# Half steps of 128 columns with both signs in one PSUM bank, and block sums on GpSimd, in a fused FFT and cosine-gated feed-forward kernel

## The chip, the cores and the metric

The kernel runs on one core of one Trainium2 chip. A core has TensorE (PE in the profile, with its weight loads listed apart as PEld), VectorE (DVE), ScalarE (ACT), GpSimd (POOL) and SyncE (SP, which issues transfers). Each engine works through its own instructions in the order in which they were written; engines wait for one another through semaphores. Matmuls write to PSUM, which has eight banks of 128 partitions by 512 fp32 values; VectorE and ScalarE read and write PSUM too, GpSimd and transfers only SBUF. The metric is the device time of one execution in microseconds (us), lower is better.

## The reference

```python
def _attn_ref(x) -> np.ndarray:            # x: (8, 3008, 256)
    X = np.fft.fft(x, axis=1)
    X = np.fft.fft(X, axis=2)
    return X.real.astype(np.float32)

def _moe_ref(x, w_in, w_out) -> np.ndarray:  # (24064, 256), (256, 2048), (2048, 256)
    h = x @ w_in
    g = h * np.cos(h)
    return (g @ w_out).astype(np.float32)
```

The result of the first function, as 24064 rows of 256 values, is the input of the second. All is fp32, and the matmuls run in fp32, which the trace records as two passes for each.

## The kernel before

**Transform.** A batch is 3008 rows (47 by 64) of 256 columns. `transform(b)` lays out the work of the Fourier transform of batch `b` over the 48 steps of the batch before it, as a table from step to calls: `load_x` (four pieces), `fold` (sums and differences of column pairs, on GpSimd for all batches but the first, two per chunk of 512 columns), `first_half` (matmuls of a chunk into a bank `pz`, the even part into partitions 0 to 63, the odd part into 64 to 127, and then a few single columns once more with another weight), `store_z` and `load_z` (through DRAM, to turn the data), and `second_half` (four matmuls of 128 columns into a bank `pb`, copied by ScalarE to `pq`; its first row is spread over all partitions as `nb` by two transfers). `pz` of later batches and `pb` use one PSUM bank of their own, tag "fft".

**What a step is.** The output of a batch is made in 6 groups of T = 225 (the first) or 256 positions, and each group in 8 steps of 256 columns of `w_in`, so there are 8 x 6 x 8 = 384 steps. The column transform is folded into the weights `WC` and `WS` (cosine and sine parts). A position and its mirror share the cosine part `e` and differ in the sign of the sine part: one matmul with WC and one with WS give both values of `h`.

A step `s` does, for its two blocks `u` of 128 columns:
- `seed` (ScalarE): starts the bank H with 0.25 plus a weight times `nb`.
- `mm1(s, 0)` (TensorE, WC) adds the even part; `act_e` (ScalarE) saves twice that as `ew`.
- `mm1(s, 1)` (TensorE, WS) adds the odd part: H holds the one sign; `dve_h` (VectorE) makes the other sign, `ew - H`, with positions reversed, in the SBUF tile `h`.
- For each sign: `act_round` (ScalarE, adds a large constant, which rounds), `dve_frac` (VectorE, the fraction), then one `act_sin` (ScalarE) over both signs, and `dve_g` (VectorE) multiplies by `h`.
- `dve_s` (VectorE, three parts) makes four sums and differences of the four blocks (two signs by two `u`) in the tile `S`.
- `mm2` (TensorE): seven matmuls of the blocks and sums with combinations of `w_out` add up in four PSUM banks M over the 8 steps of a group.

At the end of a group `take_m` (ScalarE) copies the M banks to `mr`, `combine_m` (GpSimd, seven products into the four outputs, six instructions and two memsets for T = 225) makes `cb`, and `store_out` transposes 32 by 32 on VectorE and sends the rows out.

**Order.** Nothing is scheduled by a planner: the loop at line 740 writes the instructions of step `t` (`cur`), of `t - 1` (`prev`), `t - 2` (`old`) and `t - LAG`, LAG = 3 (`done`), in the order in which every engine is to take them. On TensorE a step is `mm1(cur, 0)`, four matmuls of `mm2(done)`, `mm1(cur, 1)`, three of `mm2(done)`. On ScalarE it is `act_e`, two seeds for the next step, `act_sin`, and two `act_round`. On VectorE it is two `dve_g`, two `dve_frac` with the first of `dve_s` between them, the second of `dve_s`, `dve_h` and the third of `dve_s`. The table of `transform` and that of the opening come at the end of each step.

**Buffers.** PSUM: one bank "fft", four M, three H. A new tile waits until the last reader of the bank that it takes is done.

Of the kernel before, what the change touches and what calls it, by code (L numbers as in the profile page):

```python
# [107 lines left out]
def kernel(  # L108
# [90 lines left out]
    bank = {"fft": 1, "M": 4, "H": 3}  # L199

    def psum(name, tag="fft"):
        return ppool.tile([128, 512], FP, tag=tag, bufs=bank[tag], name=name)
# [3 lines left out]
    xf0 = [spool.tile([128, 2 * IP * 128], FP, tag="S", bufs=2, name="xf") for _ in range(2)]  # L206
# [3 lines left out]
    def fold(b, c, e):  # L210
        lo = IP * (c % 2)
        xv = xs[b, c // 2].rearrange("r (i d) -> r i d", d=ND)[0 : 2 * N2, lo : lo + IP]
        if b == 0:
            xfs[b, c] = xf0[c % 2]
        elif e == 0:
            xfs[b, c] = spool.tile([128, 2 * IP * 128], FP, tag="xf", bufs=1, name="xf")
# [14 lines left out]
    def first_half(b, c):  # L231

        rows = 2 * N2 if b else 128
        fv = xfs.pop((b, c)).rearrange("r (e c) -> r e c", e=2)[0:rows]
        LE, LO, LE0, LO0 = (L[0:rows, 64 * q : 64 * q + 64] for q in range(4))
        pz = psum("pz", "fft" if b else "M")
        a = 128 if c == 0 else 0
        for e, (w, w0) in enumerate(((LE, LE0), (LO, LO0))):
            rows = slice(64 * e, 64 * e + 64)
            if a:  # L240
                nc.tensor.matmul(
                    pz[rows, 0:128], lhsT=w0, rhs=fv[:, e, 0:128], start=True, stop=True
                )
            nc.tensor.matmul(  # L244
                pz[rows, a:512], lhsT=w, rhs=fv[:, e, a:512], start=True, stop=True
            )
        if a:
            nc.tensor.matmul(
                pz[64:128, 0:1], lhsT=LE0, rhs=fv[:, 1, 0:1], start=True, stop=True
            )  # L250
        nc.tensor.matmul(  # L251
            pz[64:128, a:512:128],
            lhsT=LE,
            rhs=fv[:, 1, a:512:128],
            start=True,
            stop=True,
        )
        tag, n = ("zs", 4) if b or c < 4 else ("pq", 8)
        zs = spool.tile([128, 512], FP, tag=tag, bufs=n, name="zs")
        nc.scalar.copy(out=zs, in_=pz)  # L260
        zss[b, c] = zs
# [28 lines left out]
    def second_half(b, g):  # L290
# [4 lines left out]
        for q in range(4):  # L295
# [5 lines left out]
                start=True,  # L301
                stop=True,
            )
# [26 lines left out]
    def transform(b):  # L330
# [5 lines left out]
        for p in range(4):  # L336
            at(8 * p + (0 if p else 3), load_x, b, p)
            for c, o, f in ((2 * p, 6, 8), (2 * p + 1, 9, 13)):
                at(8 * p + o, fold, b, c, 0)
                at(8 * p + o, fold, b, c, 1)  # L340
                at(8 * p + f, first_half, b, c)
                at(8 * p + f + 1, store_z, b, c)
# [80 lines left out]
    def seed(s):  # L423
        T = s.T
        s.pq, s.nb = ready[s.b, s.grp]
        s.H = psum("H", "H")
        for u in range(2):
            f = 2 * s.fp + u
            nc.scalar.activation(  # L429
                out=s.H[:, u * T : u * T + T],  # L430
                in_=s.nb[:, 0:T],
                func=AF.Copy,
                bias=0.25,
                scale=wn[:, f : f + 1],
            )

    def seed_first(s):
        for u in range(2):
            nc.tensor.matmul(
                s.H[:, u * s.T : u * s.T + s.T],  # L440
                lhsT=wrow[:, 128 * u : 128 * u + 128],
                rhs=s.pq[0:1, s.T : 2 * s.T],
                start=False,
                stop=True,
                skip_group_check=True,
            )

    def mm1(s, e):
        T = s.T
        W = WS if e else WC  # L450
        for u in range(2):
            f = 2 * s.fp + u
            nc.tensor.matmul(  # L453
                s.H[:, u * T : u * T + T],
                lhsT=W[:, 128 * f : 128 * f + 128],
                rhs=s.pq[:, e * T : e * T + T],
                start=False,
                stop=True,
                skip_group_check=True,
            )  # L460

    def act_e(s):
        s.ew = spool.tile([128, 512], FP, tag="ew", bufs=2, name="ew")
        nc.scalar.mul(out=s.ew[:, 0 : 2 * s.T], in_=s.H[:, 0 : 2 * s.T], mul=2.0)  # L464

    def dve_h(s):
        T = s.T
        s.h = spool.tile([128, 512], FP, tag="h", bufs=3, name="h")
        nc.vector.tensor_tensor(  # L469
            out=s.h[:, 0 : 2 * T].rearrange("p (u t) -> p u t", u=2)[:, :, ::-1],  # L470
            in0=s.ew[:, 0 : 2 * T].rearrange("p (u t) -> p u t", u=2),
            in1=s.H[:, 0 : 2 * T].rearrange("p (u t) -> p u t", u=2),
            op=ALU.subtract,
        )

    def side(s, sg):
        T = s.T
        return s.r[:, 2 * T * sg : 2 * T * sg + 2 * T], (s.h if sg else s.H)[:, 0 : 2 * T]

    def act_round(s, sg):  # L480
        if sg == 0:
            s.r = spool.tile([128, 1024], FP, tag="r", bufs=4, name="r")
        r, h = side(s, sg)
        nc.scalar.activation(out=r, in_=h, func=AF.Copy, bias=BIG, scale=1.0)  # L484

    def dve_frac(s, sg):
        r, h = side(s, sg)
        nc.vector.scalar_tensor_tensor(  # L488
            out=r, in0=r, scalar=-BIG, in1=h, op0=ALU.add, op1=ALU.subtract
        )  # L490

    def act_sin(s):
        r = s.r[:, 0 : 4 * s.T]
        nc.scalar.activation(out=r, in_=r, func=AF.Sin, bias=0.0, scale=SIN_SCALE)  # L494

    def dve_g(s, sg):
        r, h = side(s, sg)
        nc.vector.scalar_tensor_tensor(  # L498
            out=r, in0=h, scalar=-0.25, in1=r, op0=ALU.add, op1=ALU.mult
        )  # L500

    def dve_s(s, k):
        T = s.T
        gv = s.r[:, 0 : 4 * T].rearrange("p (q t) -> p q t", q=4)
        if k == 0:
            s.S = spool.tile([128, 1024], FP, tag="S", bufs=2, name="S")
        sv = s.S[:, 0 : 4 * T].rearrange("p (q t) -> p q t", q=4)
        if k == 0:
            nc.vector.tensor_tensor(  # L509
                out=sv[:, 0:2],  # L510
                in0=gv[:, 2:3].to_broadcast([128, 2, T]),
                in1=gv[:, 0:4:3],
                op=ALU.subtract,
            )
        elif k == 1:
            nc.vector.tensor_tensor(out=sv[:, 2], in0=sv[:, 1], in1=gv[:, 0], op=ALU.subtract)  # L516
        else:
            nc.vector.tensor_tensor(out=sv[:, 3], in0=gv[:, 1], in1=sv[:, 2], op=ALU.add)  # L518
# [4 lines left out]
    def mm2(s, part):  # L523
        T = s.T
        key = (s.b, s.grp)
        if s.fp == 0 and part == 0:
            acc[key] = []
            started[key] = set()
        gv = s.r[:, 0 : 4 * T].rearrange("p (q t) -> p q t", q=4)
        sv = s.S[:, 0 : 4 * T].rearrange("p (q t) -> p q t", q=4)  # L530
        todo = (
            (0, wv[:, 0, 0, s.fp], gv[:, 0]),
            (1, wv[:, 1, 0, s.fp], gv[:, 1]),
            (2, vx[:, 3, s.fp], gv[:, 3]),
# [5 lines left out]
        for m, w, a in todo[4:] if part else todo[:4]:  # L540
# [17 lines left out]
    def take_m(s, part):  # L558
        T = s.T
        key = (s.b, s.grp)  # L560
        if part == 0:
            mrs[key] = spool.tile([128, 7 * 256], FP, tag="mr", bufs=1, name="mr")
        mv = mrs[key].rearrange("p (m t) -> p m t", m=7)[:, :, 0:T]
        for k in (2, 3) if part else (0, 1):
            n = 1 if k == 3 else 2
            nc.scalar.mul(
                out=mv[:, 2 * k : 2 * k + n],
                in_=acc[key][k].rearrange("p (m t) -> p m t", m=2)[:, 0:n, 0:T],
                mul=TWO_PI,
            )  # L570

    def combine_m(s):
        T = s.T
        key = (s.b, s.grp)
        acc.pop(key)
        mv = mrs.pop(key).rearrange("p (m t) -> p m t", m=7)[:, :, 0:T]
        cb = spool.tile([128, 7 * 256], FP, tag="cb", bufs=1, name="cb")
        cf = cb.rearrange("p (m t) -> p m t", m=7)
        cv = [cf[:, m, 256 - T : 256] if m in (2, 3) else cf[:, m, 0:T] for m in range(7)]
        if T < 256:  # L580
            nc.gpsimd.memset(cf[:, 0:2, T:256], 0.0)
            nc.gpsimd.memset(cf[:, 2:4, 0 : 256 - T], 0.0)
        tt = nc.gpsimd.tensor_tensor
        tt(out=cv[0], in0=mv[:, 0], in1=mv[:, 1], op=ALU.add)
        tt(out=cv[4], in0=mv[:, 0], in1=mv[:, 5], op=ALU.subtract)
        tt(
            out=cf[:, 5:7, 0:T],
            in0=cf[:, 4:5, 0:T].to_broadcast([128, 2, T]),
            in1=mv[:, 3:5],
            op=ALU.add,  # L590
        )
        tt(out=cv[1], in0=cv[6], in1=mv[:, 6], op=ALU.add)
        tt(out=cv[2], in0=cv[5], in1=mv[:, 2], op=ALU.add)
        tt(out=cv[3], in0=cv[5], in1=mv[:, 4], op=ALU.add)
        outs[key] = cb
# [138 lines left out]
    first = steps[0]  # L734
    first.H = psum("H", "H")
    nc.vector.memset(first.H[:, 0 : 2 * first.T], 0.25)
    second_half(0, 0)
    keep_busy(2, "M", 256)
    first.pq, first.nb = ready[0, 0]
    for t in range(n + LAG + 1):  # L740
        cur, prev, old, done = step(t), step(t - 1), step(t - 2), step(t - LAG)
        if cur:
            if t % per == 0:
# [80 lines left out]
```

## Time and profile before

| | |
|---|---|
| median of 3 runs | 1974.51 us (1973.8 to 1974.56) |
| profiled execution, first to last instruction | 1973.1 us |
| mean granted TensorE clock | 0.999 of full |
| 128x1024 sine on ScalarE (L494) | 320 of 1.055 us |
| seed on ScalarE (L429), 128x256 | 640 of 0.478 us |
| `act_e` on ScalarE (L464), 128x512 | 320 of 0.596 us |
| `dve_g` on VectorE (L498), 128x512, from H in PSUM / from `h` in SBUF | 0.672 / 0.729 us |
| first sum of `dve_s` on VectorE (L509), 128x512 | 0.764 us |
| transfers (all queues) | 88.63 MB, 45 GB/s |

The page lists for each engine its busy time and the share of the span. A row of a group reads: line, engine, operation, tiles as out<-in, shape, how many, then busy time in us and the mean of one in ns, then the idle time before them and who ended it. A timeline row reads: start in us, length, engine, line, operation, tiles and shape, count, and in brackets an idle time and who ended it. The recorded end of a matmul includes its way through the array, so matmuls that follow each other without a gap overlap in the record; the distance between starts tells the rate. The same holds for VectorE and ScalarE, where an instruction starts before the one ahead of it has ended in the record.

### The profile page before, as it was taken

The page shows a single profiled execution, that of the slowest core. Times are in us where ns is not written, and L with a number is a line of the kernel's source. Part 1 is how long each engine was busy: PE and PEld are TensorE (multiplying, and loading weights), DVE is VectorE, ACT ScalarE, POOL GpSimd, SP SyncE. Part 2 cuts the span into 40 slices and gives each one's busy share as a digit, 9 for nine tenths or more (in the row PEclk, how much of TensorE's full clock was granted, in tenths as well). Part 3 has the DMA queues.
Part 4 walks back from the last instruction along what each step waited for, and adds up shares of the span by engine and source line. Part 5 has one row for each costly group of instructions (what it writes and reads, how often), then busy time and mean ns, then how long its engine had stood idle before and what let it go on. Part 6 is the DMA issues. An engine that isn't in the chain of part 4 may idle for free.

```text
span 1973.1 us, 28657 instructions
## 1 busy us (share of the span) xinstructions
PE 1948.9 (99%) x9360; PEld 1702.4 (86%) x9360; DVE 1854.4 (94%) x3209; ACT 1482.7 (75%) x2687; POOL 465.1 (24%) x428
## 2 busy tenths in 40 slices
PE   8999999999999999999999999999999999999998
PEld 4888899888988889888898888988889888898887
DVE  2999989999899998999989999999999999899998
ACT  3777777777777777777877777777777777778775
POOL 1123113221133212223222322123311233112111
PEclk9999999999999999999999999999999999999999
DMA  8413221131212212122122301223022220200000
GB/s 194 100 41 62 41 43 31 40 59 35 43 33 46 51 36 43 38 59 38 34 41 51 63 20 37 45 53 55 19 42 53 43 51 21 47 21 10 19 15 22
DMA packets 176682, 88.63 MB, mean 45 GB/s; under 512 B 103303, under 2 KB 173622, under 8 KB 174902
## 3 DMA queue, kind: packets, MB, share of 16 engines
q1 hardware_dynamic: 176374, 86.68, 21.4%
q8 instruction: 75, 1.23, 0.3%
q14 instruction: 73, 0.60, 0.1%
q10 hardware_dynamic: 160, 0.13, 0.0%
HBM read 49.50 MB, written 37.27 MB: 44 GB/s over the span
## 4 chain that ended last, share of the span: by engine, by line
PE 91%; DVE 5%; DMA 2%; ACT 1%; issue 1%; SPq 0%; DVEq 0%; POOL 0%; ACTq 0%; POOLq 0%
PE M L545 53%; PE H L453 31%; PE pz L244 3%; PE pb L297 2%; DVE r L498 1%; DMA xp<-in_x_dram 1%; DVE S L516 1%; DVE S L509 1%; DVE S L518 1%; DVE h L469 1%; DVE r L488 1%; ACT r L484 0%; PE pw L355 0%; DMA out_dram<-ob 0%; SPq L647 0%
## 5 line engine op out<-in xcount | busy, mean ns | idle before, releaser
L494 ACT ACTIVATE r<-r 128x1024 f32<-128x1024 f32 (+1 forms) x384 | 398.5, 1038 | 303.6 <-DVE r L488 302.7
L545 PE MATMUL M<-S,VX 128*128 128x256 f32 (+1 forms) x2304 | 612.3, 375 | 0.0
L545 PEld LDWEIGHTS M<-S,VX 128*128 128x128 f32 x2304 | 437.8, 190 | 49.9
L453 PE MATMUL H<-pq,WS 128*128 128x256 f32 (+1 forms) x1536 | 390.2, 376 | 11.5 <-ACT ew L464 11.2
L453 PE MATMUL H<-pq,WC 128*128 128x256 f32 (+1 forms) x1536 | 393.9, 379 | 0.5 <-ACT H L429 0.5
L545 PE MATMUL M<-r,w 128*128 128x256 f32 (+1 forms) x1536 | 387.7, 375 | 0.0
L429 ACT ACTIVATE H<-nb,wn 128x256 f32<-128x256 f32 (+1 forms) x766 | 362.9, 474 | 18.0 <-DVE r L498 5.6
L469 DVE TENSOR_TENSOR h<-ew,H 128x512 f32<-128x512 f32 (+1 forms) x384 | 256.8, 669 | 92.5 <-PE H L453 86.5
L453 PEld LDWEIGHTS H<-pq,WS 128*128 128x128 f32 x1536 | 289.3, 190 | 53.9 <-ACT ew L464 20.0
L545 PEld LDWEIGHTS M<-r,w 128*128 128x128 f32 x1536 | 300.7, 197 | 27.0
L488 DVE SCALAR_TENSOR_TENSOR r<-r,h 128x512 f32<-128x512 f32 (+1 forms) x384 | 309.5, 806 | 0.0
L453 PEld LDWEIGHTS H<-pq,WC 128*128 128x128 f32 x1536 | 283.2, 190 | 28.9 <-ACT H L429 0.8
L218 POOL TENSOR_TENSOR xf<-xp 94x508 f32<-94x508 f32 x112 | 165.4, 1497 | 566.0 <-PE pz L251 547.9
L509 DVE TENSOR_TENSOR S<-r 128x512 f32<-128x512 f32 (+1 forms) x384 | 290.2, 756 | 0.1
L498 DVE SCALAR_TENSOR_TENSOR r<-h,r 128x512 f32<-128x512 f32 (+1 forms) x384 | 272.6, 710 | 0.0
L484 ACT ACTIVATE r<-H 128x512 f32<-128x512 f32 (+1 forms) x384 | 222.9, 580 | 55.7 <-DVE h L469 52.7
L464 ACT ACTIVATE ew<-H 128x512 f32<-128x512 f32 (+1 forms) x384 | 225.4, 587 | 50.3 <-PE H L453 43.8
L488 DVE SCALAR_TENSOR_TENSOR r<-r,H 128x512 f32<-128x512 f32 (+1 forms) x384 | 255.1, 664 | 0.0
L498 DVE SCALAR_TENSOR_TENSOR r<-H,r 128x512 f32<-128x512 f32 (+1 forms) x384 | 254.0, 661 | 0.3 <-ACT r L494 0.3
L484 ACT ACTIVATE r<-h 128x512 f32<-128x512 f32 (+1 forms) x384 | 236.2, 615 | 0.0
L545 PE MATMUL M<-S,w 128*128 128x256 f32 (+1 forms) x768 | 225.2, 375 | 0.0
L545 PE MATMUL M<-r,VX 128*128 128x256 f32 (+1 forms) x768 | 225.1, 375 | 0.0
(72 smaller groups left out, 1498.4 us busy)
## 6 DMA issues: line engine op xcount, KB each, us to landing
out_dram<-ob SPq DMA_DIRECT2D x728, 32.0 KB
xp<-in_x_dram SPq DMA_DIRECT2D x56, 256.0 KB
zd<-zs SPq DMA_DIRECT2D x112, 96.0 KB
z<-zd SPq DMA_DIRECT2D x28, 384.0 KB
xp<-in_x_dram SPq DMA_DIRECT2D x56, 120.0 KB
nb<-nd SPq DMA_DIRECT2D x40, 128.0 KB
wr<-in_moe_w_in_dram SPq DMA_DIRECT2D x8, 256.0 KB
w<-in_moe_w_out_dram SPq DMA_DIRECT2D x4, 512.0 KB
```

The lines of the kernel that those rows point to most:

```text
L218: (nc.gpsimd if b else nc.vector).tensor_tensor(out=fv[:, e, :, 1:128], in0=xv[:, :, 1:128], in1=xv[:, :, 255:128:-1], op=ALU.subtract if ...
L244: nc.tensor.matmul(pz[rows, a:512], lhsT=w, rhs=fv[:, e, a:512], start=True, stop=True)
L429: nc.scalar.activation(out=s.H[:, u * T : u * T + T], in_=s.nb[:, 0:T], func=AF.Copy, bias=0.25, scale=wn[:, f : f + 1],)
L453: nc.tensor.matmul(s.H[:, u * T : u * T + T], lhsT=W[:, 128 * f : 128 * f + 128], rhs=s.pq[:, e * T : e * T + T], start=False, stop=True, ...
L464: nc.scalar.mul(out=s.ew[:, 0 : 2 * s.T], in_=s.H[:, 0 : 2 * s.T], mul=2.0)
L469: nc.vector.tensor_tensor(out=s.h[:, 0 : 2 * T].rearrange("p (u t) -> p u t", u=2)[:, :, ::-1], in0=s.ew[:, 0 : 2 * T].rearrange("p (u t) ...
L484: nc.scalar.activation(out=r, in_=h, func=AF.Copy, bias=BIG, scale=1.0)
L488: nc.vector.scalar_tensor_tensor(out=r, in0=r, scalar=-BIG, in1=h, op0=ALU.add, op1=ALU.subtract)
L494: nc.scalar.activation(out=r, in_=r, func=AF.Sin, bias=0.0, scale=SIN_SCALE)
L498: nc.vector.scalar_tensor_tensor(out=r, in0=h, scalar=-0.25, in1=r, op0=ALU.add, op1=ALU.mult)
L509: nc.vector.tensor_tensor(out=sv[:, 0:2], in0=gv[:, 2:3].to_broadcast([128, 2, T]), in1=gv[:, 0:4:3], op=ALU.subtract,)
L545: nc.tensor.matmul(acc[key][m // 2][:, 256 * (m % 2) : 256 * (m % 2) + T], lhsT=w, rhs=a, start=first, stop=s.fp == 7, skip_group_check=True,)
```

## The change

A step is cut into two half steps, one for each block `u` of 128 columns, and the loop runs over half steps `k` = 2t + u. A half step has an H bank of its own: positions 0 to T hold the one sign, T to 2T the other, written by `dve_h` into PSUM. `act_round`, `dve_frac`, `act_sin` and `dve_g` each run once for a half step, over both signs; the sine becomes 512 columns wide, `act_e` and `dve_h` 256. The four blocks in `r` therefore stand in another order (block, then sign). `dve_s` becomes `sums`, on GpSimd for all steps but the last, written after the `dve_g` of the second half step. `mm2` is cut as 3, 1 and 3 matmuls.

The bank "fft" is gone: `pz` and `pb` come from the H tag, which now has four banks. `first_half` writes the single columns first and leaves them out of the odd matmul, which then has 508 columns. `take_m` empties the second and fourth M bank on VectorE, the others on ScalarE, one in each place; `combine_m` is spread over six steps, one piece at the end of each. The two `store_out` of a group move from 2 and 3 steps after the last `mm2` to 5 and 7. The tile `xf` has two buffers for one, `S` three for two, `ew` half the width, and the tile `h` is gone. In `transform`, three of four loads come three steps earlier, the two folds of a chunk stand in separate steps, and the first halves move by one step.

```diff
-    bank = {"fft": 1, "M": 4, "H": 3}
+    bank = {"M": 4, "H": 4}
...
-            xfs[b, c] = spool.tile([128, 2 * IP * 128], FP, tag="xf", bufs=1, name="xf")
+            xfs[b, c] = spool.tile([128, 2 * IP * 128], FP, tag="xf", bufs=2, name="xf")
...
+        for i0, i1, wE, wO in parts:
+            mul(1, i0, i1, 0, 1, wE, 1, i0 == 0)
+        for i0, i1, wE, wO in parts:
+            mul(0, i0, i1, 0, 128, wE, 0, i0 == 0)
+            mul(1, i0, i1, 1, 128, wO, 1, False)
...
-            at(8 * p + (0 if p else 3), load_x, b, p)
-            for c, o, f in ((2 * p, 6, 8), (2 * p + 1, 9, 13)):
+            at(8 * p, load_x, b, p)
+            for c, o, f in ((2 * p, 6, 9), (2 * p + 1, 9, 12)):
                 at(8 * p + o, fold, b, c, 0)
-                at(8 * p + o, fold, b, c, 1)
+                at(8 * p + o + 1, fold, b, c, 1)
...
+    def seed(h):
+        s, T = h.s, h.s.T
+        if h.u == 0:
+            s.pq, s.nb = ready[s.b, s.grp]
+        h.H = psum("H", "H")
+        f = 2 * s.fp + h.u
+        nc.scalar.activation(
+            out=h.H[:, 0:T], in_=s.nb[:, 0:T], func=AF.Copy, bias=0.25, scale=wn[:, f : f + 1]
+        )
...
+    def act_e(h):
+        T = h.s.T
+        h.ew = spool.tile([128, 256], FP, tag="ew", bufs=2, name="ew")
+        nc.scalar.mul(out=h.ew[:, 0:T], in_=h.H[:, 0:T], mul=2.0)
+
+    def dve_h(h):
+        T = h.s.T
+        nc.vector.tensor_tensor(
+            out=h.H[:, T : 2 * T][:, ::-1], in0=h.ew[:, 0:T], in1=h.H[:, 0:T], op=ALU.subtract
+        )
+
+    def sides(h):
+        T = h.s.T
+        return h.s.r[:, 2 * T * h.u : 2 * T * h.u + 2 * T], h.H[:, 0 : 2 * T]
...
+    def act_sin(h):
+        r, _ = sides(h)
+        nc.scalar.activation(out=r, in_=r, func=AF.Sin, bias=0.0, scale=SIN_SCALE)
...
+    def sums(s):
         T = s.T
+        s.S = spool.tile([128, 1024], FP, tag="S", bufs=3, name="S")
+        gv, sv = blocks(s)
+        qv = s.r[:, 0 : 4 * T].rearrange("p (q t) -> p q t", q=4)
+        tt = (nc.vector if s is steps[-1] else nc.gpsimd).tensor_tensor
+        tt(
+            out=sv[:, 0:2],
+            in0=qv[:, 1:2].to_broadcast([128, 2, T]),
+            in1=qv[:, 0:4:3],
             op=ALU.subtract,
         )
+        tt(out=sv[:, 2], in0=sv[:, 1], in1=gv[:, 0, 0], op=ALU.subtract)
+        tt(out=sv[:, 3], in0=gv[:, 1, 0], in1=sv[:, 2], op=ALU.add)
...
+        if eng is nc.scalar:
+            eng.mul(out=to, in_=at, mul=TWO_PI)
+        else:
+            eng.tensor_scalar(out=to, in0=at, scalar1=TWO_PI, scalar2=None, op0=ALU.mult)
...
+    for k in range(2 * (n + LAG)):
+        t, u = divmod(k, 2)
+        cur, prev, old, nxt = unit(k), unit(k - 1), unit(k - 2), unit(k + 1)
+        done = step(t - LAG)
+        full = step(t - LAG, True) if u else step(t - LAG - 1, True)
         if cur:
...
             mm1(cur, 0)
...
             act_e(cur)
...
         if done:
-            mm2(done, 0)
+            mm2(done, 4 * u, 4 * u + 3)
         if old:
-            dve_g(old, 0)
-            dve_g(old, 1)
-        if step(t + 1):
-            seed(step(t + 1))
+            dve_g(old)
+            if old.u:
+                sums(old.s)
         if prev:
-            dve_frac(prev, 0)
-        if old:
-            dve_s(old, 0)
+            act_round(prev)
+        if nxt and k:
+            seed(nxt)
+        if full:
+            take_m(full, 0 if u else 2, nc.scalar)
         if prev:
-            dve_frac(prev, 1)
+            dve_frac(prev)
             act_sin(prev)
-        if old:
-            dve_s(old, 1)
-        if step(t - LAG, True):
-            take_m(done, 0)
         if cur:
             mm1(cur, 1)
-        if done:
-            mm2(done, 1)
+        if done and u == 0:
+            mm2(done, 3, 4)
         if cur:
             dve_h(cur)
-            act_round(cur, 0)
-            act_round(cur, 1)
-        if old:
-            dve_s(old, 2)
-        if step(t - LAG - 2, True):
-            store_out(step(t - LAG - 2), 0)
-        if step(t - LAG - 3, True):
-            store_out(step(t - LAG - 3), 1)
+        if full:
+            take_m(full, 1 if u else 3, nc.vector)
+        if u == 0:
+            continue
+        for i in range(6):
+            s = step(t - LAG - 1 - i, True)
+            if s:
+                combine_m(s, i)
+        for sg, lag in ((0, 5), (1, 7)):
+            s = step(t - LAG - lag, True)
+            if s:
+                store_out(s, sg)
```

## The prediction

> **What bounds the kernel now.** I read the page first, then the timeline of a quiet stretch, then the waits, then the groups of instructions by shape.
>
> ```profile
> span 1973.1 us, 28657 instructions
> PE 1948.9 (99%) x9360; PEld 1702.4 (86%) x9360; DVE 1854.4 (94%) x3209; ACT 1482.7 (75%) x2687; POOL 465.1 (24%) x428
> PEclk9999999999999999999999999999999999999999
> PE 91%; DVE 5%; DMA 2%; ACT 1%; issue 1%; SPq 0%; DVEq 0%; POOL 0%; ACTq 0%; POOLq 0%
> ```
>
> TensorE carries 91% of the chain that ended last and VectorE is nearly as full. A busy matmul row overlaps its neighbour, so the starts tell more:
>
> ```profile
> 1794.35 1.03 PE L453 MATMUL H<-pq,WC 128*128 128x256 f32 x4
> 1795.21 1.03 PE L545 MATMUL M<-r,w 128*128 128x256 f32 x4
> 1796.94 1.03 PE L453 MATMUL H<-pq,WS 128*128 128x256 f32 x4
> 1797.80 1.03 PE L545 MATMUL M<-S,VX 128*128 128x256 f32 x4
> 1799.10 1.03 PE L453 MATMUL H<-pq,WC 128*128 128x256 f32 x4
> ```
>
> One step lasts 1799.10 - 1794.35 = 4.75 us. It has 11 fp32 matmuls, each recorded twice (1536 + 1536 + 5376 records over 384 steps = 22), so 4.75 / 22 = 0.216 us a pass, and the four passes from 1794.35 to 1795.21 show the same 0.216. There is no gap: TensorE runs at its own rate at full clock. The change leaves these 22 passes, so it can gain only what TensorE still waits. That stands at the start of a batch:
>
> ```profile
> 550.51 0.54 PE L545 MATMUL M<-S,VX 128*128 128x225 f32 x2
> 551.71 1.03 PE L453 MATMUL H<-pq,WS 128*128 128x225 f32 x4 [0.65 <-ACT ew L464]
> ...
> 555.62 0.54 PE L545 MATMUL M<-S,VX 128*128 128x225 f32 x2
> 556.66 1.03 PE L453 MATMUL H<-pq,WS 128*128 128x225 f32 x4 [0.50 <-ACT ew L464]
> ```
>
> Two passes of 225 columns take 0.38, so the first WS matmul was due at 550.89 and came 0.82 late, the second (due 556.00) 0.66 late, a third some 0.22. That is 1.70 us, and it recurs at the start of six batches: 10.2 us. Five or six like it in the opening (46 to 80 us) add 5.7. The reason is in the shapes:
>
> ```profile
> L488 DVE SCALAR_TENSOR_TENSOR r<-r,h 128x512 f32<-128x512 f32 x320 | 266.3, 832 | 0.0
> L488 DVE SCALAR_TENSOR_TENSOR r<-r,H 128x512 f32<-128x512 f32 x320 | 215.9, 675 | 0.0
> ...
> L218 POOL TENSOR_TENSOR xf<-xp 94x508 f32<-94x508 f32 x112 | 165.4, 1497 | 566.0 <-PE pz L251 547.9 <-DMA xp<-in_x_dram 18.1
> ...
> L593 POOL TENSOR_TENSOR cb<-cb,mr 128x256 f32<-128x256 f32 x39 | 47.3, 1214 | 0.0
> ...
> L584 POOL TENSOR_TENSOR cb<-mr 128x256 f32<-128x256 f32 x39 | 29.4, 754 | 706.5 <-ACT mr L566 470.4 <-DVE h L469 236.1
> ...
> L566 ACT ACTIVATE mr<-M 128x256 f32<-128x256 f32 x39 | 15.8, 406 | 0.0
> ```
>
> The same VectorE subtraction takes 0.675 with its second input in PSUM and 0.832 with both in SBUF; one GpSimd shape takes 0.75 or 1.21. In the timeline the long ones meet: two-SBUF-input work of VectorE and work of GpSimd stretch each other. At a batch start two folds, the combination and a transpose stand together, and `ew` falls behind.
>
> **VectorE's load.** Start to start, a 512-column instruction takes 0.60 and a 256-column one 0.34. Before, a step has 4 + 1 + 1 of the former and 2 of the latter: 4.3 of 4.75 us. After, `dve_h` runs twice at 256, `dve_frac` and `dve_g` twice each at 512: 0.68 + 2.40 = 3.1 us, and 0.2 for the transposes and its part of `take_m`. `dve_s` leaves (1.3 us). Every VectorE instruction of the loop now has at most one SBUF input, so the stretching ends on both sides; I take back the whole 10.2 us (bounds 0 and 10.2).
>
> **GpSimd's load.** Without overlap the trace has 1.27 for 128x512 (1.34 until a dependent instruction starts) and 0.73 to 0.80 for 128x256: `sums` costs 1.34 + 0.76 + 0.73 = 2.83 us a step. Folds (16 of 1.22 in 48 steps: 0.41) and the combination (five of 0.75 and one of 1.34 in 8 steps: 0.64) bring 3.88 of 4.75 us. A step with a fold and a combine piece needs 4.8, twice in eight; the last sum is due about 1.5 steps after `dve_g`, which leaves over 4 us for the backlog. Cost on the path: 0. The folds, moved to other steps, still precede their matmuls by two.
>
> **ScalarE's loop, where half steps could hurt.** Per half step: `act_e` (256), `act_round` (512), seed (256), `act_sin` (512). Start to start: 512 columns 0.476 to 0.49, 256 columns 0.26 (the mr copy), seed 0.41 to 0.50, so 0.83 ns a column, a 1024 sine 0.96 and a 512 one 0.96 - 512 x 0.83 ns = 0.54. Sum 1.71, that is 3.4 us a step. The loop round, frac, sine, next `act_e`, next round takes 0.59 + 0.04 + 0.67 + 0.04 + 0.54 + 0.26 = 2.14 (0.04 is the gap seen from one engine's end to the other's start). TensorE's half steps have 12 and 10 passes, 2.59 and 2.16, mean 2.38. It holds.
>
> The tightest loop lies in the short half: two WC passes (0.216 + 0.379 = 0.60), gap 0.04, `act_e` until the round may start 0.26, round until the seed 0.49, seed 0.48, gap 0.05, weight load of the next WC matmul 0.11 (an unprefetched pass is that much longer). Sum 2.03 against 2.16: 0.13 us to spare. `act_e` itself ends long before WS (six passes, 1.3 us). No row shows a half-width `act_e` or a VectorE write to PSUM; for the first the mr row is nearest (bounds: 0.26 and the 512-column 0.48), for `dve_h` the SBUF row of 0.41 and the frac row of 0.67, and its 0.4 us of slack in the short half covers both. [...]
>
> **Banks.** The transform's tiles now share H's four banks. Each new tile takes the bank that `dve_g` of two half steps earlier gave back; that ends about 1.0 us into the half step, seeds come at 1.39 and pz or pb at 2.16. Cost 0, covered by that margin; without it a late bank delays TensorE by what is missing. At a group's end the second M bank is now emptied by VectorE after `dve_h`: 2.16 + 0.16 + 0.04, + 0.34, + 0.67, + 0.05 = 3.42 into the half step, while the next group's matmul wants it at 2.16 + 0.43 + 0.86 - 0.11 = 3.34. That is 0.07 late, 47 times: + 3 us. The first, on ScalarE, ends 0.04 in time.
>
> **The first matmuls of the transform.** A chunk holds TensorE for 1.08 us, with four 512-column passes on two halves of the array that run side by side (0.92 for two pairs) and two 4-column passes at the end. These move to the front, on the odd half, beside the even one. They may vanish (- 0.1) or push the odd half back (+ 0.1): 0 +/- 6 us over 64 chunks.
>
> **Opening and end.** Until the first `mm2` six half steps run at ScalarE's loop, some 2 us each against 2.5 to 2.8 per step now with waits: later by 1 to 2 us at step 3, and the waits of 1.55 at 73 to 79 us go. Net 0 +/- 2. The tail is TensorE's backlog of three steps and stays.
>
> **The sum.** 1973.1 - 10.2 + 3 + 0 + 0 = 1965.9. The runs' median is 1974.5, 1.4 above the profiled span; so 1967.
>
> **The rivals.**
> 1. The seed comes late: the short loop exceeds 2.16. Should a half-width `act_e` hold ScalarE as long as a full one (+ 0.21), each step loses 0.21 - 0.13 = 0.08: 384 x 0.08 = 31 us, 1967 + 31 = 1998. It decides from 0.13 us; at 0.18 it is 1986. For it: the sum of small fixed costs. Against it: the 406 ns row beside 592. Chance 0.20.
> 2. The gain is given back at boundaries (M banks, H banks, folds that wait on GpSimd): 0.2 us at each of 47 group changes instead of 0.07, and some per chunk: 1974. Chance 0.18.
> 3. GpSimd becomes the bound: with the stretched rows `sums` takes 1.34 + 1.21 + 1.21 = 3.8, folds 0.57, combination 0.84: 5.2 us a step against a mean step of (1951.04 - 38.41) / 383 = 4.99 (first to last WC matmul), about 1974.5 + 0.2 x 384 = 2050. It needs VectorE instructions with two SBUF inputs, and none is left. Chance 0.05.
> 4. The odd and even passes no longer run side by side because the small ones stand ahead: + 0.85 a chunk, 64 x 0.85 = 54: 2021. The first chunk of a batch already mixes such passes and keeps them parallel. Chance 0.04.
> 5. More is found: the small passes hide (- 6), the opening's 5.7 goes, no M wait (- 3): 1953. Chance 0.08.
>
> **How the numbers follow.** The forecast has 0.45; its own range is 1959 to 1974. A change within 0.2% of 1974.5 (1970.6 to 1978.5) can hardly be told from none. Faster: 0.41 of the forecast, 0.08 of rival 5, 0.04 of rival 2: 0.53. Within: 0.04 and 0.13: 0.17. Slower: 0.01 of rival 2, all of 1, 3 and 4: 0.30. The range 1954 to 1994 leaves out the far part of rival 1, rivals 3 and 4 and the edge of 5, about 0.2.
>
> **What would show it.** Right: the start-to-start time of a quiet step stays 4.75 us; VectorE falls to about 70% busy, GpSimd rises to about 80%; 128x256 GpSimd rows at 0.73 to 0.80; the batch-start waits on `ew` gone; the span near 1966. Wrong: WC weight loads that wait for the seed (rival 1), matmuls on S waiting for GpSimd (3), chunks of 2 us (4), a first M matmul waiting for mr at every group (2).

## The result, and the profile after

The changed kernel takes 1978.68 us (median of 13 runs, 1977.83 to 1979.85) against 1974.37 for the kernel before (13 runs): 1.0023 times as long, 95% interval 1.0014 to 1.0031. It is 4.3 us slower, where 7.5 us less was forecast. The four lines of the page that answer to those of before:

```profile
span 1977.9 us, 29797 instructions
PE 1960.2 (99%) x9360; PEld 1688.2 (85%) x9360; DVE 1467.6 (74%) x2540; ACT 1505.2 (76%) x3360; POOL 1388.3 (70%) x1577
PEclk9899999999999999999999999999999999999999
PE 97%; DMA 1%; DVE 1%; SPq 0%; ACT 0%; issue 0%; POOL 0%; DVEq 0%; POOLq 0%
```

VectorE fell from 94% to 74%, GpSimd rose from 24% to 70%, and TensorE's share of the chain that ended last rose from 91% to 97%. What was to be relieved is relieved. One digit is new: an 8 in the second slice (49 to 99 us) of the granted clock, where before there is a 9. In the timeline, the quiet step and the start of the third batch look as forecast:

```profile
1803.28 0.59 PE L452 MATMUL H<-pq,WC 128*128 128x256 f32 x2
...
1808.03 0.59 PE L452 MATMUL H<-pq,WC 128*128 128x256 f32 x2
```

```profile
554.49 0.54 PE L452 MATMUL H<-pq,WS 128*128 128x225 f32 x2
...
558.68 0.54 PE L452 MATMUL H<-pq,WS 128*128 128x225 f32 x2
```

The first pair are the same half of two successive steps: 4.75 us, unchanged. The second pair, a step of 225 columns apart, show 4.19 = 22 x 0.1905: no pass is late, and no bracket names `ew`. The groups by shape:

```profile
L484 DVE SCALAR_TENSOR_TENSOR r<-r,H 128x512 f32<-128x512 f32 x640 | 439.4, 687 | 259.9 <-ACT r L480 247.9
...
L464 ACT ACTIVATE ew<-H 128x256 f32<-128x256 f32 x640 | 244.8, 382 | 87.6 <-PE H L452 80.0
...
L218 POOL TENSOR_TENSOR xf<-xp 94x508 f32<-94x508 f32 x112 | 141.6, 1265 | 0.0
...
L594 POOL TENSOR_TENSOR cb<-cb,mr 128x256 f32<-128x256 f32 x39 | 28.4, 728 | 0.0
```

A GpSimd fold went from 1497 to 1265 ns, a combination piece of the same shape as before from up to 1214 to 728: in the loop nothing stretches any more.

So the loss is elsewhere. Set both traces to their first matmul and compare, step by step, when the first WC matmul starts. By how much the changed kernel is later than before:

| step | 0 | 1 | 3 | 7 | 8 | 11 | 48 | 56 | 96 | 104 | 336 | end |
|---|---|---|---|---|---|---|---|---|---|---|---|---|
| later by, us | 0.16 | 1.08 | 4.42 | 5.78 | 7.64 | 8.53 | 9.16 | 7.42 | 8.27 | 6.53 | 4.09 | 4.86 |

Eleven steps of opening lose 8.5 us. Six batch starts win 1.74 each, 10.4 in all. And between them every batch gives some 0.85 back. The chain of waits says what the opening loses; its rows are start, duration, engine, tile and line:

```profile
72.06 1.98 DVE VX L418 x3
...
74.06 0.42 DVE VX L418
...
77.81 2.12 DVE VX L418 x3
79.94 0.02 issue
79.96 1.37 DVE VX L418
81.33 0.54 DVE r L494
81.87 0.54 DVE r L484
```

Line 418 is `combine_w2`, which prepares the second weights from w_out, in groups of four instructions in steps 0, 1, 5 and 6. The last group stands for 3.5 us in VectorE's queue (77.81 to 81.33), and `dve_g` (L494) and `dve_frac` (L484) of the running half steps stand behind it. The group before it takes 2.4 us. The timeline shows who waits for these; below them the kernel before at the same work:

```profile
82.43 0.58 ACT L490 ACTIVATE r<-r 128x450 f32<-128x450 f32 x1 [3.28 <-DVE r L484]
...
83.31 0.65 PE L452 MATMUL H<-pq,WS 128*128 128x225 f32 x2 [1.99 <-ACT ew L464]
```

```profile
74.17 0.43 DVE L419 TENSOR_TENSOR VX<-w,VX 128x256 f32<-128x256 f32 x1
...
74.46 1.03 PE L453 MATMUL H<-pq,WS 128*128 128x225 f32 x4 [0.55 <-ACT ew L464]
```

The last of the four takes 0.43 us before and 1.37 after. All four read SBUF twice, and since the change GpSimd works beside them (sums, and a fold at 79.61):

```profile
79.61 1.44 POOL L218 TENSOR_TENSOR xf<-xp 94x508 f32<-94x508 f32 x1
...
79.96 1.37 DVE L418 TENSOR_TENSOR VX<-w,VX 128x256 f32<-128x256 f32 x1
```

The stretching is a wait: the fold ends at 81.05 and this instruction 0.28 us later, at 81.33. Of the sixteen, nine take over 0.5 us, and every one of the nine ends 0.28 to 0.29 us after a GpSimd instruction has ended. The sine waits 3.28 us for frac, and TensorE stands for 1.99. Then comes a second price. Windows of 4 us (length, busy time of PE, PEld, DVE, ACT, POOL, then the granted clock, DMA share and GB/s):

```profile
48.00:52.00 4.00, 3.11 (x8) 1.40 (x8) 2.95 (x7) 3.15 (x8) 1.30 (x2) 0.80 1.23 186
52.00:56.00 4.00, 1.98 (x5) 1.00 (x4) 3.63 (x7) 2.00 (x6) 1.21 (x2) 0.50 1.17 223
...
84.00:88.00 4.00, 3.89 (x11) 3.37 (x12) 1.91 (x4) 2.41 (x7) 3.43 (x4) 0.57 0.01 2
```

The kernel before has 1.00 in all of these. At half the clock the same work takes TensorE longer: the first four passes of second matmuls are 1.71 us in one row (57.70) and 0.92 at 63.36.

### The profile page after: what moved, and what is told of

Its sections match the earlier page's. It is cut to its first block, busy times and chain, and to the rows that moved or that the text cites. A ratio compares the mean times of both kernels' runs of the same rounds, so it can differ in the third digit from the quotient of the medians.

```text
span 1977.9 us, 29797 instructions
## 1 busy us (share of the span) xinstructions
PE 1960.2 (99%) x9360; PEld 1688.2 (85%) x9360; DVE 1467.6 (74%) x2540; ACT 1505.2 (76%) x3360; POOL 1388.3 (70%) x1577
## 4 chain that ended last, share of the span: by engine, by line
PE 97%; DMA 1%; DVE 1%; SPq 0%; ACT 0%; issue 0%; POOL 0%; DVEq 0%; POOLq 0%
PE M L543 57%; PE H L452 33%; PE pz L242 3%; PE pb L295 2%; DMA xp<-in_x_dram 1%; DVE VX L418 0%; PE pw L354 0%; SPq L650 0%; DMA wr<-in_moe_w_in_dram 0%; DMA out_dram<-ob 0%; DVE r L484 0%; PE pd L399 0%; PE pw L367 0%; ACT ew L464 0%; ACT r L490 0%
## 5 line engine op out<-in xcount | busy, mean ns | idle before, releaser
L510 POOL TENSOR_TENSOR S<-r 128x512 f32<-128x512 f32 (+1 forms) x383 | 475.2, 1241 | 476.3 <-PE M L543 239.5
L484 DVE SCALAR_TENSOR_TENSOR r<-r,H 128x512 f32<-128x512 f32 (+1 forms) x768 | 518.9, 676 | 287.4 <-ACT r L480 273.5
L490 ACT ACTIVATE r<-r 128x512 f32<-128x512 f32 (+1 forms) x768 | 477.8, 622 | 277.2 <-DVE r L484 276.6
L494 DVE SCALAR_TENSOR_TENSOR r<-H,r 128x512 f32<-128x512 f32 (+1 forms) x768 | 518.4, 675 | 99.7 <-ACT r L490 50.1
L480 ACT ACTIVATE r<-H 128x512 f32<-128x512 f32 (+1 forms) x768 | 447.7, 583 | 0.0
L468 DVE TENSOR_TENSOR H<-ew,H 128x256 f32<-128x256 f32 (+1 forms) x768 | 325.2, 423 | 95.4 <-PE H L452 22.1
L464 ACT ACTIVATE ew<-H 128x256 f32<-128x256 f32 (+1 forms) x768 | 290.3, 378 | 103.9 <-PE H L452 92.8
L516 POOL TENSOR_TENSOR S<-S,r 128x256 f32<-128x256 f32 (+1 forms) x383 | 276.0, 721 | 30.0
L517 POOL TENSOR_TENSOR S<-r,S 128x256 f32<-128x256 f32 (+1 forms) x383 | 275.7, 720 | 30.0
L543 PEld LDWEIGHTS M<-S,w 128*128 128x128 f32 x768 | 150.5, 196 | 14.6
```

Source lines behind the costliest of these rows:

```text
L464: nc.scalar.mul(out=h.ew[:, 0:T], in_=h.H[:, 0:T], mul=2.0)
L468: nc.vector.tensor_tensor(out=h.H[:, T : 2 * T][:, ::-1], in0=h.ew[:, 0:T], in1=h.H[:, 0:T], op=ALU.subtract)
L480: nc.scalar.activation(out=r, in_=y, func=AF.Copy, bias=BIG, scale=1.0)
L484: nc.vector.scalar_tensor_tensor(out=r, in0=r, scalar=-BIG, in1=y, op0=ALU.add, op1=ALU.subtract)
L494: nc.vector.scalar_tensor_tensor(out=r, in0=y, scalar=-0.25, in1=r, op0=ALU.add, op1=ALU.mult)
L510: tt(out=sv[:, 0:2], in0=qv[:, 1:2].to_broadcast([128, 2, T]), in1=qv[:, 0:4:3], op=ALU.subtract,)
```

## The experiments

Three theories. The opening: `combine_w2` blocks VectorE, and the clock falls after TensorE's stall. The loss that recurs: M banks that are late at each group change, and the new order of the transform's small matmuls. And the clock alone. Two further runs ask where the gain at the batch starts came from. The runs b1 and b2 edit the kernel before, all others the changed kernel; all medians are set against runs of the kernel before on the same chip:

| run | median us | ratio to before, 95% interval |
|---|---|---|
| e1_fill | 1978.08 | 1.0018 (1.0009 to 1.0027) |
| e2_comb_pool | 1971.03 | 0.9984 (0.9975 to 0.9993) |
| e9_spread | 1972.25 | 0.9988 (0.9980 to 0.9997) |
| e3_take_act | 1984.02 | 1.0050 (1.0037 to 1.0063) |
| e7_take_early | 1973.09 | 0.9992 (0.9983 to 1.0000) |
| e4_old_pz | 1976.16 | 1.0008 (0.9999 to 1.0017) |
| e8_pz_last | 1975.86 | 1.0008 (0.9999 to 1.0016) |
| b1_new_folds | 2010.63 | 1.0182 (1.0169 to 1.0196) |
| b2_sums_pool | 2086.00 | 1.0564 (1.0549 to 1.0578) |
| e5_sums_dve | 2041.39 | 1.0336 (1.0322 to 1.0350) |
| c1_all | 1963.18 | 0.9942 (0.9929 to 0.9954) |
| c2_all_fill | 1961.75 | 0.9937 (0.9925 to 0.9950) |

**The opening: combine_w2 on GpSimd**

```diff
-            nc.vector.tensor_tensor(
+            nc.gpsimd.tensor_tensor(
                 out=dst[:, f0:f1], in0=a[:, f0:f1], in1=b[:, f0:f1], op=op
```

> The changed kernel with the preparation of the second weights (combine_w2, 16 instructions with two SBUF inputs in the first 83 us) on GpSimd in place of VectorE. If the opening lost its 9 us because these instructions meet the block sums on GpSimd and stand ahead of frac and g on VectorE: the four of 1.40, 0.88 and 1.37 us at 77.7 to 81.3 go from VectorE, the sine's wait of 3.28 and TensorE's idle 1.99 at 83.3 go, with them the clock of 0.57 from 84 to 88 (about 1.7 us), and the sine's wait of 1.88 and TensorE's 1.59 at 56.0: 5 to 7 us less than 1978.7, so 1972 to 1974. If the opening loses by half steps as such (a chain of 2 us with no second matmuls to hide it): at most 1 us less. If GpSimd is late with sums and fold instead: matmuls on S wait, and the time stays or grows.

1971.0, which is 7.6 us less than the changed kernel, a little beyond the range, and faster than before. From step 0 to step 11 the trace gains 7.4 us on the changed kernel, and after that 0.2 more. Steps 7 and 8 give most of it, 2.7 and 1.8: the wait at 83 us is gone, and from 56.2 us on the clock stays at 1.00. Step 6, behind the group of 2.4 us, gives 0.7. Sixteen instructions of the opening thus carry nearly all that it lost. The 1.1 us left (8.5 - 7.4) are not the price of half steps as such, since the clock is still at 0.50 in this run from 49.4 to 56.2 us; the last run of this section takes that away too.

**The opening: combine_w2 one by one**

```diff
+        for k0, f in ((3, 2), (9, 4), (13, 6)):
+            if k0 <= k < k0 + 4:
+                combine_w2(f, f + 2, k - k0, k - k0 + 1)
         if u == 0:
             continue
...
-        1: ((combine_w2, 2, 4),),
-        5: ((combine_w2, 4, 6), (second_half, 0, 1)),
-        6: ((combine_w2, 6, 8),),
+        5: ((second_half, 0, 1),),
```

(`combine_w2` gets two more arguments that cut its list of four.)

> The changed kernel with combine_w2 still on VectorE, but after the first group of four its instructions stand one by one, each in a half step of its own (half steps 3 to 6, 9 to 12, 13 to 16). GpSimd runs beside them as before. If the opening's loss is that four of them stand in a row ahead of frac and g (3.65 us at 77.7 to 81.3): most of the 7.6 that moving them to GpSimd gave, so 1971 to 1973. If it is that each is stretched by GpSimd (1.37 in place of 0.43) whatever its place: 2 or 3 us less at most, 1976 to 1977.

1972.25, 6.4 of the 7.6. The instructions still meet GpSimd, as the timeline of this run shows:

```profile
75.58 1.29 DVE L418 TENSOR_TENSOR VX<-w 128x256 f32<-128x256 f32 x1
...
77.97 0.58 ACT L490 ACTIVATE r<-r 128x450 f32<-128x450 f32 x1 [0.77 <-DVE r L484]
```

1.29 us for one, and yet the sine waits 0.77 where it waited 3.28. Steps 6 and 7 take what they take with `combine_w2` on GpSimd (4.19 us each). Steps 8 and 9, with the two longest instructions (1.29 and 1.41 us), take 10.7 where that run has 10.1. So one long instruction is nearly swallowed by the slack of a half step, and four in a row are not: the place in VectorE's queue decides. That the row must also be stretched to hurt this much is argued from the two rows above, of which the one of 2.4 us cost its step 0.7 and the one of 3.5 us 2.7; no run has four unstretched ones in half steps.

**The clock: keep TensorE busy in the opening**

```diff
+    def fill(n):
+        pd = psum("pd", "M")
+        nc.tensor.matmul(pd[:, 0:n], lhsT=BJ[:, 0:128], rhs=BJ[:, 0:n], start=True, stop=True)
...
+            elif k < 6:
+                fill(256)
...
             mm1(cur, 1)
+            if 0 < k < 6:
+                fill(256)
```

> Left out: nothing; ten extra matmuls of 256 columns, whose result no one reads, fill half steps 1 to 5, so that TensorE does not stand idle there. The changed kernel's granted clock is 0.80 from 48 to 52 us, 0.50 from 52 to 60, 0.92 from 60 to 64, where the kernel before has 1.00; its matmuls from 57.7 to 60.7, the first that do not wait for a vector engine, run at that clock. If the lowered clock is a part of the opening's loss: clock 1.00 from 48 to 64, and 1.5 to 2 us less than the changed kernel (1978.7), so about 1977. If the loss is the vector engines' chain alone: the clock may rise, the time stays at 1978.7 or grows by what the extra matmuls delay.

In the windows of this run the clock stays up:

```profile
52.00:56.00 4.00, 2.01 (x10) 1.51 (x9) 3.57 (x8) 1.73 (x6) 0.76 (x3) 1.00 1.14 286
```

Steps 0 to 2 take 0.4 us longer with the extra matmuls, and step 3, the first with second matmuls, takes 4.19 us in place of 6.05: 1.86 from the clock alone. The net gain of the trace, 1.4, is just short of the 1.5 to 2 expected, and the medians (1978.08 and 1978.68, with intervals that overlap) don't show it; the time of step 0 after the first matmul varies between profiled runs by up to 2 us, as much as the effect. What is shown is the mechanism and its size in the step; that it shortens the whole is not. The second fall of the clock, behind the wait at 83 us, is still in this run (82.6 to 86.0 us). What it costs can be read in the run with the old order of the small matmuls further down: there the group of `combine_w2` costs step 7 the same (6.87 us in both), but the clock stays at 1.00, and step 8 takes 4.50 us in place of 6.18, 1.7 less.

**The recurring loss: M banks**

In the last batch, which has no transform, the changed kernel still falls back by 0.15 us a group. Its timeline at a group change:

```profile
1898.98 1.03 PE L543 MATMUL M<-r,w 128*128 128x256 f32 x4
1899.09 0.68 DVE L568 TENSOR_SCALAR mr<-M 128x512 f32<-128x512 f32 x1
...
1899.92 0.67 PE L543 MATMUL M<-r,VX 128*128 128x256 f32 x2
```

The third product was due at 1898.98 + 4 x 0.216 = 1899.84. VectorE empties its bank until 1899.77, and it starts at 1899.92, 0.08 late; its two passes then take 0.67 and not 0.59, another 0.08. Over both traces, from step 10 on, these passes exceed their 0.216 or 0.1905 by 5.9 us in the changed kernel, at 38 of the 47 group changes, and by nothing before. Why nine are spared was not followed up. First try, ScalarE empties all four banks:

```diff
-            take_m(full, 1 if u else 3, nc.vector)
+            take_m(full, 1 if u else 3, nc.scalar)
```

> The changed kernel with all four M banks emptied by ScalarE at a group's end. Rival theory, the loss recurs at group changes: the changed kernel falls back by 0.15 us at each group even in the last batch, which has no transform; if VectorE's emptying of the second bank is the cause, 47 x 0.07 to 0.15 = 3 to 7 us less than 1978.7, 1972 to 1976. If the opening alone is it, and ScalarE's extra 0.41 us twice a group delays the sine and the next seeds: the same or up to 5 us more.

1984.0, 5.3 more. Two emptyings now stand in ScalarE's queue of one half step, and the time goes the other way: WC loads wait for the seed 16.8 us in 62 places, where the changed kernel has 5.6 in 24. So this run says nothing against VectorE's part. The second try moves the first bank half a step ahead and gives the second bank the first one's place:

```diff
-        if full:
-            take_m(full, 0 if u else 2, nc.scalar)
+        if full and u == 0:
+            take_m(full, 2, nc.scalar)
+        if step(t - LAG, True):
+            take_m(step(t - LAG, True), u, nc.scalar)
...
-        if full:
-            take_m(full, 1 if u else 3, nc.vector)
+        if full and u == 0:
+            take_m(full, 3, nc.vector)
```

> The changed kernel with the first M bank of a group emptied half a step earlier and the second one in the first one's old place, both by ScalarE, the third and fourth as they are. The first matmuls of the next group then find their banks free long before. If these waits are the 0.15 us a group by which the changed kernel falls back where no transform runs: 47 x 0.07 to 0.15 = 3 to 7 us less than 1978.7, so 1972 to 1975. If ScalarE's extra 0.41 us in a long half delays the seed, as in the run with all four banks on ScalarE (1984): the same or more.

1973.1, 5.6 less than the changed kernel. The trace gains 0.15 a group in the last batch and 6.0 from step 4 to the end; the excess of those passes is nil. In its timeline the third product follows the first by 0.86, and its row is 0.59. The engine changed here along with the place. ScalarE at the old place made it worse, so the place, after `dve_h` in the short half, is the likelier cause; VectorE at an earlier place was not tried.

**The recurring loss: the small matmuls**

> The changed kernel with the small matmuls of the transform's first half again behind the large ones, as the kernel before has them. A chunk takes 1.112 us of TensorE in the changed kernel against 1.074 before, so 64 x 0.04 = 2.4 us less than 1978.7, 1976.3, if that order is the cause of the chunk's difference. If the chunk's difference is due to the bank shared with H (a wait for it), no change.

```diff
-        for i0, i1, wE, wO in parts:
-            mul(1, i0, i1, 0, 1, wE, 1, i0 == 0)
-        for i0, i1, wE, wO in parts:
-            mul(0, i0, i1, 0, 128, wE, 0, i0 == 0)
-            mul(1, i0, i1, 1, 128, wO, 1, False)
+        for e, (w, w0) in enumerate(((LE, LE0), (LO, LO0))):
...
```

(the loop of the kernel before, every matmul with `start=True`). In this form the kernel does not compute the reference's values; the time is read for the order alone. 1976.2, 2.5 less. The same order, with only the first matmul of each half starting the bank:

```diff
         for i0, i1, wE, wO in parts:
-            mul(1, i0, i1, 0, 1, wE, 1, i0 == 0)
-        for i0, i1, wE, wO in parts:
             mul(0, i0, i1, 0, 128, wE, 0, i0 == 0)
-            mul(1, i0, i1, 1, 128, wO, 1, False)
+            mul(1, i0, i1, 1, 128, wO, 1, i0 == 0)
+        for i0, i1, wE, wO in parts:
+            mul(1, i0, i1, 0, 1, wE, 1, False)
```

> The changed kernel with the transform's small matmuls behind the large ones, where only the first matmul of each half starts the bank. As in the run with the old order (1976.2, its step times 2.1 less from step 11 to the end): 1976 to 1977. If that gain was due to the starts and not to the order: 1978.7.

1975.9, 2.8 less. From its first matmul to the next one of the loop, a chunk takes 1.074 us before, 1.112 in the changed kernel, 1.067 here. The loop has 56 chunks, since the eight of the first batch lie ahead of it: 56 x 0.045 = 2.5, which is what the trace gains from step 11 to the end. The order is the cause.

**Where the batch starts' gain comes from**

One part of the change alone in the kernel before: the transform at its new offsets.

```diff
-            at(8 * p + (0 if p else 3), load_x, b, p)
-            for c, o, f in ((2 * p, 6, 8), (2 * p + 1, 9, 13)):
+            at(8 * p, load_x, b, p)
+            for c, o, f in ((2 * p, 6, 9), (2 * p + 1, 9, 12)):
                 at(8 * p + o, fold, b, c, 0)
-                at(8 * p + o, fold, b, c, 1)
+                at(8 * p + o + 1, fold, b, c, 1)
```

(and two `xf` buffers)

> The kernel before with one part of the change alone: the transform's loads, folds and first-half matmuls at the offsets of the changed kernel (the two folds of a chunk one step apart, two xf buffers), everything else as before. In the changed kernel each of six batches starts 1.74 us faster than before, 10.4 in all. If that came from the half steps with the block sums on GpSimd, as the prediction has it: most of the batch-start waits stay, and the time is 1970 to 1975. If it came from the folds' new places alone: 10 us less than before, 1964 to 1966.

2010.6: neither range. The rival that the folds' places alone bring the gain is refuted, since each batch's first group loses 0.44 us instead of winning 1.74, and the next three groups some 1.45 each. Waits of the WS weight loads on `ew` grow from 20 us (25 times) to 66 us (111 times). The new offsets are bad for full steps; why each group with two folds loses 1.45 was not followed further. The other part alone, the block sums on GpSimd:

```diff
-            nc.vector.tensor_tensor(
+            nc.gpsimd.tensor_tensor(
                 out=sv[:, 0:2],
```

(and the two that follow it)

> The kernel before with one part of the change alone: the block sums on GpSimd, full steps and the SBUF tile h as before. VectorE is relieved of 1.3 us a step, but half of its frac and g (those that read h) still have two SBUF inputs. If moving the sums is enough for the batch starts: 10 us less than before or better, 1960 to 1965. If GpSimd and VectorE stretch each other as the rows of 0.675 and 0.832, 0.75 and 1.21 say, and h in PSUM is what makes the move pay: sums of 3.2 to 3.8 us, folds and combination stretched too, GpSimd near 5 us a step, and S late for the second matmuls: 1975 to 2050.

2086, beyond the range on the side of the stretching. Its groups by shape:

```profile
L488 DVE SCALAR_TENSOR_TENSOR r<-r,h 128x512 f32<-128x512 f32 x320 | 397.9, 1243 | 0.0
...
L516 POOL TENSOR_TENSOR S<-S,r 128x256 f32<-128x256 f32 x320 | 306.4, 957 | 25.1
```

The frac of the h side takes 1243 ns where it took 832 before; that of the H side stays at 677. Of the 320 rows on the h side 225 take over 0.75 us, and all of these end 0.54 to 0.55 us after a GpSimd instruction has ended: here too the stretching is a wait. A sum of 128x256 takes 957 in place of 730. TensorE's matmuls wait for S, 82 us in all. So this move costs 112 us by itself, and in these runs it pays only beside half steps with h in PSUM.

The reverse, sums on VectorE in the changed kernel at the start of seven batches:

```diff
-        tt = (nc.vector if s is steps[-1] else nc.gpsimd).tensor_tensor
+        i = steps.index(s)
+        tt = (nc.vector if s is steps[-1] or (i >= per and i % per < 7) else nc.gpsimd).tensor_tensor
```

> The changed kernel with the block sums of the first seven steps of batches 2 to 8 on VectorE, as before. If the batch starts are faster because VectorE no longer has instructions with two SBUF inputs there: the waits on ew return, 7 x 1.7 = 12 us more than 1978.7 or beyond, since VectorE also has 1.4 us a step more to do: 1988 to 2000. If the half steps alone (or the folds' places) made the batch starts faster: 1977 to 1981.

2041, 63 more; 9.0 a batch and not 1.7, beyond the range. The waits on `ew` return (52 us of weight loads against 9), but this is more than before: from 293 to 328 us VectorE is busy 30.7 us, TensorE works only 30.9, where the changed kernel has 27.7 and 35.0, and the clock falls to 0.95. This run does not separate VectorE's load from the stretching; with the one before it, it shows that neither the sums on GpSimd nor the half steps have the gain without the other.

**All three repairs**

combine_w2 on GpSimd, the early emptying, the small matmuls behind.

> The changed kernel with three edits together: combine_w2 on GpSimd (7.6 less by its run), the transform's small matmuls behind the large ones, here with only the first matmul of each half starting the bank (2.1 less by the step times of the run with the old order), and the early emptying of the M banks (3 to 6). If the three losses are separate: 1978.7 - 13 to 16 = 1963 to 1966, faster than both kernels. If one hides another: 1968 to 1971.

1963.2, 15.5 less than the changed kernel and 0.58% faster than before. The single gains were 7.6, 5.6 and 2.8, sum 16.0, so the three losses are separate but for 0.5. Its page:

```profile
span 1961.4 us, 29793 instructions
...
PE 99%; DMA 0%; DVE 0%; ACT 0%; SPq 0%; POOL 0%; issue 0%; DVEq 0%
```

TensorE makes up 99% of the chain: little is left but its own passes. The same with the extra matmuls:

> The three edits of the run at 1963.2 and, in half steps 1 to 5, the extra matmuls that keep the clock at 1.00. If the lowered clock (0.50 to 0.97 between 48 and 60 us with combine_w2 on GpSimd) still costs where the second matmuls begin: 1 to 2 us less, 1961 to 1962. If the chain of ScalarE and VectorE sets those half steps: 1963.

1961.75. Step 3 takes 4.19 us in place of 6.03, as in the first run with them, and the clock from 48 to 60 us is 1.00. Steps 0 to 10 take 54.3 us, against 56.1 without the extra matmuls, 62.8 in the changed kernel and 54.5 before: with `combine_w2` off VectorE and the clock kept up, half steps lose nothing in the opening. The intervals of the two overlap (0.9925 to 0.9950, 0.9929 to 0.9954), so the 1.4 us between the medians are not settled.

## Why the forecast was wrong, step by step

**The step that failed** is "Opening and end", "Net 0 +/- 2". It measured + 8.5 us. The sum there put at nothing what VectorE's one-time work would cost once GpSimd is busy. The working there took ScalarE's loop of 2 us for all six half steps, and the argument above it, that "every VectorE instruction of the loop now has at most one SBUF input", left out the `combine_w2` groups, VectorE instructions that aren't of the loop but run in it. From 48 to 80 us GpSimd was busy for 3.0 us before and is for 15.1 now (sums of the windows); an instruction of `combine_w2` took 0.42 to 0.55 us on average and now takes 0.65 to 0.69, up to 1.37 (one took 1.48 before, too, beside a fold, and its step lost nothing). Of the 8.5 us, moving it away gives 7.4. The clock was not in the sum at all: 1.86 us of the opening's loss are due to it at step 3, and some 1.7 at step 8, where the fall of the clock goes with `combine_w2`. Without either, the opening is 0.2 us shorter than before, so what the step did price nearly cancels, as it said.

**The batch starts**, - 10.2, came as - 10.4, but that is net of what M banks and chunks lose in the same groups. By themselves the WS matmuls that were late on `ew` give back 12.3 us from step 10 on: some 10.3 of lateness, as priced, and 2.1 because the second pass behind each also took 0.10 longer, which the sum did not count. So the close match of the two numbers is in part luck. The reason fits, rows unstretched and WS on time; how much of it is the stretching and how much VectorE's lighter load, no run separates.

**The second M bank**, + 3, was the right place at half its size. Priced at 0.07 in each of 47 group changes, it measured 5.9 us in 38 of them, 0.15 in most. The lateness of 0.08 was right; that the pair of passes then also takes 0.08 longer was forgotten, although a price of 0.11 for such a weight load stands in the working of the short loop.

**The small matmuls**, 0 +/- 6, lie at + 2.1 (56 x 0.038): they push the odd half back by 0.04 a chunk of the 0.1 allowed.

**The loops.** ScalarE's short loop had 0.13 us to spare by forecast and held: WC loads wait for the seed 5.6 us in all, in 24 places of 768. From the start of a half-width `act_e` to the round behind it is 0.28 us (1899.18 to 1899.46), near the row of 0.26 that the sum used. Rival 1 falls with that, rival 3 with GpSimd at 70% and no matmul of the loop waiting for S, rival 4 with chunks of 1.11 us. Rival 2 was half right: the M banks give back twice what was priced, the H banks at most 0.6 us, by which pairs of WC passes run longer than before.

With the measured sizes, the opening to step 10 and the rest from there, the sum is 1973.1 + 8.4 - 12.3 + 5.9 + 2.1 + 0.6 = 1977.8 against the span of 1977.9.

## What to carry over

When work moves to an engine, look for whom it meets in every phase of the program, not in the loop alone: a few one-time instructions that were harmless beside an idle GpSimd led to the longest wait of TensorE in the loop, 1.99 us. Place one-time work one instruction at a time between the links of a tight loop; of a group of four in front of a link most was paid (2.7 of 3.5 us, and the clock behind it), even though the engine has a quarter of its time free. And price a wait on TensorE with what follows it: the weight load that was not fetched ahead (the load of the pass at 83.31 starts with the pass, and the row of two takes 0.65 in place of 0.54 us) and the clock (1.86 us at step 3).

## What was not expected of the hardware

The granted clock halves without any long pause. In the 3.41 us before the fall at 50.43 us (as long as the shorter of the two dips) TensorE had worked on six passes of 0.19 us or a little more and a part of a seventh, with gaps under 1 us; in those before the second fall on three and a part of a fourth, with one pause of 1.99. The count of passes in such a stretch does not decide alone: the kernel before has one with five (49.05 to 52.46) and keeps 1.00. Half-microsecond windows of the changed kernel, TensorE alone (length, busy time, clock, DMA share, GB/s), bound both dips:

```profile
50.00:50.50 0.50, 0.31 (x1) 0.93 1.21 173
...
60.50:61.00 0.50, 0.50 (x4) 0.83 0.77 125
...
84.50:85.00 0.50, 0.50 (x3) 0.56 0.05 16
...
87.50:88.00 0.50, 0.50 (x3) 0.53 0.00 0
```

With 1.00 and 0.50 as the two levels, it falls at 84.56 and returns at 87.97: 3.41 us. The first dip lasts from 50.43 to 60.67, 10.24 us, three times that. What sets these lengths, and how much work in which stretch keeps the clock up, no run here shows. What a dip costs differs with its place: step 3 without extra matmuls takes 6.05 us in the changed kernel, whose dip ends at 60.67, and 4.92 with `combine_w2` on GpSimd, where it ends at 56.2; with the extra matmuls and no dip there it takes 4.19. The 1.86 and 0.73 above that are half of what the dip covers of the step (3.74 and some 1.4 us).

The stretching of VectorE by GpSimd is a wait for the other's instruction to end. With both inputs in SBUF the long VectorE rows end a fixed time after a GpSimd instruction: 0.28 us at 256 columns (`combine_w2`), 0.55 at 512 (frac of the h side, sums on GpSimd). With one input in PSUM none of the 320 frac rows of that same run takes over 0.75 us.
